# A half step of the frequency stage: all four products ahead of ScalarE's two copies

## The chip, the cores and the metric

One core of a Trainium2 chip runs the whole program in one launch. The metric is the device time of that launch in microseconds (us), the median of several runs. Engines are called by the names of the profile: PE is TensorE's matmuls (PEld its weight loads), DVE is VectorE, ACT is ScalarE, POOL is GpSimd, SP is SyncE, which issues most DMAs.

## The reference, cut to what matters

Two parts follow each other: a long convolution by Fourier transforms, and on its result a mixture of experts. The change lies in the first part:

```python
h_filt = h_mlp * window                       # S = 11456 positions, D = 128 channels
u = x * v                                     # B = 4 sequences
L = 2 * S
Uf = np.fft.rfft(u, n=L, axis=1)
Hf = np.fft.rfft(h_filt, n=L, axis=0)
y = np.fft.irfft(Uf * Hf[None, :, :], n=L, axis=1)[:, :S, :]
return (x * y).astype(np.float32)
```

Everything is float32. The second part (`_moe_ref`) picks rows of that result, sends each through one of 8 experts, and is not touched.

## The kernel before, in words

The transforms are matrix products. The sequence is cut into 3 blocks of 60 x 64 positions, and the 128 channels into 4 slices (`h`) of 32. A first stage (`first_phase`) transforms the filter and the data of slice 0 along 60 points and writes the results to DRAM (`x1f`, `x1d`). The frequency stage (`freq_phase`) reads them back. Its loop runs over 60 steps `n` (`ALL`), 15 for each slice, and every step treats four of the 60 frequencies, as two half steps `j` of two frequencies each.

One half step goes through four engines:

- `spread` (L385 to L399), called through `begin`: on PE, the products with the table `c2` take the data and the filter (`x1`, 480 columns) into frequency. There are four products of 64 output rows, two (`p` = 0, 1, which fill the lower and upper 64 partitions) for the real part (`c` = 0) and two for the imaginary part (`c` = 1). In the trace every one of them is two instructions of PE, so a group of two products is a row of "x4", two pairs that run side by side. Both groups write one PSUM tile `xp` of two banks, bank `c` for part `c`; there are two such tiles, `xp0` and `xp1`, one for each half step. ACT then copies each part to `xx` in SBUF (480 columns of the real, 384 of the imaginary part).
- `join` (L401): DVE adds the imaginary part in PSUM to the copied real part (L405), and forms the same sum of the filter (L407).
- `mult` (L410): DVE multiplies data with filter, three times (L414: `y`, `p1`, `p2`). It reads `xp` in PSUM, so the tile is free for the half step's next turn only behind the third.
- once per step, POOL adds `p1` and `p2` to `y` (L487, L488), and PE goes back from frequency (`back`, L429) one step later, in two parts (0 to 2, and 2 to 3, of the three blocks); ACT copies the result (L432), and SP stores it (`zd`, L441).

The data of the slices 1 to 3 goes through the first transform inside the frequency stage too, as pieces between the steps (`piece`, `others`): POOL multiplies x by v (L192), PE makes the products (L209), ACT copies them (L211) and issues the store to `x1d` (L197). The PSUM tiles `ps` of these pieces and of `back` come from one pool of four buffers (`qps`).

The order on each engine is the order in which the program is written (the schedule is manual); a layer that records tiles adds the waits on semaphores. On PE a step reads: `begin(n+1, 0)`, a piece, `back(0, 2)` of step n-1, `begin(n+1, 1)`, the other pieces that are due, `back(2, NB)`. The loads of `x1` (L381, L382) are issued by SP three steps ahead, into four buffers (`QX`). After the frequency stage the output stage (`out_phase`) makes the last transform, the routing and the experts.

Of the kernel before, what the change touches and what calls it, by code (L numbers as in the profile page):

```python
# [319 lines left out]
def freq_phase(tc, nc, i, fi, zd, c3, spare, loads):  # L320
# [9 lines left out]
    with (  # L330
# [9 lines left out]
        def c2(k, n=1):  # L340
            t, k = (spare, k) if k < HERE else (rest, k - HERE)
            return t[:, k * 128:(k + n) * 128]
# [42 lines left out]
        def spread(n, j):  # L385

            x1 = xs[n]
            xp = qpx.tile([128, 2, 512], F32, name=f"xp{j}")  # L390
            xx = qp.tile([128, NV, (NS + NB) * DH], F32, name=f"xx{j}", bufs=1)
            for c in range(2):
                for p in range(KH):
                    k = j * KH + p
                    nc.tensor.matmul(xp[p * 64:(p + 1) * 64, c, 0:(NS + NB) * DH],  # L395
                                     c2(n % PER * KS + k)[:, c * 64:(c + 1) * 64], x1[:, k], start=True, stop=True)
                w = (NS + NB * (1 - c)) * DH
                nc.scalar.copy(xx[:, 2 * c, 0:w], xp[:, c, 0:w])  # L398
            xps[n, j] = xp, xx  # L399
# [53 lines left out]
        def begin(n, j):  # L453
            if n < ALL:
                spread(n, j)
# [1014 lines left out]
```

## Time and profile before

| | us |
|---|---|
| median of 3 runs | 1673.21 |
| lowest and highest of them | 1672.59, 1675.7 |
| profiled execution, its own time | 1668.35 |
| its span, first to last instruction | 1666.6 |
| PE busy in that span | 1506.9 |
| DVE, POOL, ACT busy | 1059.1, 965.2, 805.6 |

The profile is one execution. The frequency stage stands from about 139 to 788 us in it. The queries used are the page itself, the waits of an engine (who stood still, and what ended it), the timeline (instructions in order of start), and windows (busy time of every engine in a stretch, with the clock granted to PE and the load of the DMA engines). In a timeline, the number in brackets is the idle time of the engine before the row and what ended it.

### The profile page before, as it was taken

How to read it: one execution, taken by the hardware profiler on the slowest of the kernel's cores; microseconds unless marked ns; L12 is line 12 of the kernel's file. 1: busy time of each engine (PE TensorE's matmuls, PEld its weight loads, DVE VectorE, ACT ScalarE, POOL GpSimd, SP SyncE). 2: the span in 40 equal slices, each digit the busy share in tenths (PEclk: the TensorE clock that was granted, in tenths of full speed). 3: DMA queues.
4: the chain of work that ended last, by engine and by line, in shares of the span. 5: the costliest groups of instructions: out<-in, count | busy, mean ns of one | idle time of the engine just before them, and what ended most of it. 6: DMA issues, size and time to landing. Idle time of an engine off the chain costs nothing. (4 is left out here: it accounts for less than half of the span.)

```text
span 1666.6 us, 27694 instructions
## 1 busy us (share of the span) xinstructions
PE 1506.9 (90%) x9149; PEld 891.9 (54%) x9149; DVE 1059.1 (64%) x2356; ACT 805.6 (48%) x1643; POOL 965.2 (58%) x808
## 2 busy tenths in 40 slices
PE   7994888888888888887789999999998999999997
PEld 3551333333333333233246776667676788888887
DVE  1324666666666667777386766667676877777773
ACT  4552554545545443333235455454544555555554
POOL 0103666666666655554036645953886788888755
PEclk9996999999999999999899999999999999999999
DMA  9999999999899988995797777877842111111100
GB/s 321 320 345 349 320 336 322 334 302 306 295 332 307 288 228 230 308 243 173 269 327 235 241 235 216 260 236 235 245 121 51 38 45 46 45 45 44 43 26 27
DMA packets 199255, 362.18 MB, mean 217 GB/s; under 512 B 64476, under 2 KB 138730, under 8 KB 199070
## 3 DMA queue, kind: packets, MB, share of 16 engines
q1 hardware_dynamic: 173430, 272.15, 50.5%
q10 hardware_dynamic: 10192, 52.51, 9.4%
q0 software_dynamic: 15488, 35.74, 7.6%
q8 instruction: 73, 1.20, 0.3%
q14 instruction: 72, 0.59, 0.1%
HBM read 216.89 MB, written 145.42 MB: 217 GB/s over the span
## 5 line engine op out<-in xcount | busy, mean ns | idle before, releaser
L740 POOL DMA_INDIRECT out<-o,ids x182 | 197.3, 1084 | 148.7 <-DVE o L747 112.2
L487 POOL TENSOR_TENSOR y<-y,p 128x1536 f32<-128x1536 f32 x59 | 203.3, 3445 | 117.4 <-DVE p L414 117.3
L429 PE MATMUL ps<-y,c 64*128 64x256 f32 (+1 forms) x1440 | 257.6, 488 | 0.4 <-POOL y L490 0.3
L669 POOL DMA_INDIRECT xt<-out,ids x182 | 192.2, 1056 | 48.4 <-issue 24.3
L398 ACT COPY xx<-xp 128x480 f32<-128x480 f32 x240 | 124.8, 520 | 176.7 <-PE xp L395 169.2
L405 DVE TENSOR_TENSOR xx<-xp,xx 128x384 f32<-128x384 f32 x120 | 66.9, 558 | 225.4 <-ACT xx L398 225.3
L882 DVE SCALAR_TENSOR_TENSOR hh<-hp,hh 128x1024 fp32r<-128x1024 f32 (+1 forms) x124 | 150.0, 1210 | 79.4 <-ACT hh L881 79.2
L429 PEld LDWEIGHTS ps<-y,c 64*128 64x128 f32 x1440 | 136.9, 186 | 114.2 <-issue 72.1
L395 PE MATMUL xp<-x,wf 128*64 128x480 f32 x512 | 135.3, 608 | 58.9 <-ACT xx L398 43.4
L432 ACT COPY z<-ps 128x512 f32<-128x512 f32 x240 | 103.6, 482 | 151.2 <-PE ps L429 151.2
L881 ACT ACTIVATE hh<-hp 128x1024 fp32r<-128x1024 f32 (+1 forms) x124 | 127.6, 1029 | 90.1 <-PE hp L736 87.1
L414 DVE TENSOR_TENSOR p<-xp,xx 128x768 f32<-128x768 f32 x240 | 169.3, 746 | 0.0
L192 POOL TENSOR_TENSOR wf<-wf 124x768 f32<-124x768 f32 x45 | 81.8, 1819 | 144.6 <-PE ps L209 109.6
L414 DVE TENSOR_TENSOR y<-xp,xx 128x1152 f32<-128x1152 f32 x120 | 162.8, 1357 | 4.1
L395 PE MATMUL xp<-x,c 128*64 128x480 f32 x448 | 114.9, 592 | 38.9 <-ACT xx L398 38.9
L211 ACT COPY wf<-ps 120x384 f32<-120x384 f32 x256 | 109.5, 486 | 47.2 <-PE ps L209 43.5
L1127 PE MATMUL y<-zt,c 128*64 128x512 f32 x384 | 110.6, 642 | 19.5 <-issue 11.0
L642 POOL MEMSET idle<- 128x512 f16 x226 | 122.5, 542 | 0.3
L209 PE MATMUL ps<-wf,c 60*120 60x384 f32 x512 | 118.5, 529 | 4.0 <-DVE wf L192 4.0
L824 PEld LDWEIGHTS bank<-wd,h 128*128 128x128 f32 x896 | 104.2, 191 | 32.8 <-issue 25.9
L620 POOL DMA_INDIRECT lists<-pl,lies x32 | 50.8, 1589 | 117.0 <-DVE step L1225 52.2
L824 PE MATMUL bank<-wd,h 128*128 128x128 f32 x896 | 114.5, 281 | 1.3 <-DVE o L747 1.3
(180 smaller groups left out, 2882.3 us busy)
## 6 DMA issues: line engine op xcount, KB each, us to landing
wf<-xv SPq DMA_DIRECT2D x64, 768.0 KB
x1d<-wf ACTq DMA_DIRECT2D x64, 720.0 KB
x<-x1d SPq DMA_DIRECT2D x60, 768.0 KB
zt<-zd SPq DMA_DIRECT2D x60, 768.0 KB
zd<-z SPq DMA_DIRECT2D x108, 384.0 KB
out<-xm SPq DMA_DIRECT2D x96, 258.0 KB
ox<-xo SPq DMA_DIRECT2D x96, 256.0 KB
x1f<-fx POOLq DMA_DIRECT2D x16, 720.0 KB
```

Of the source, the lines that this page charges most:

```text
L209: nc.tensor.matmul(ps[p], self.c1[rows], u[rows, q * RUN:(q + 1) * RUN], start=True, stop=True)
L395: nc.tensor.matmul(xp[p * 64:(p + 1) * 64, c, 0:(NS + NB) * DH], c2(n % PER * KS + k)[:, c * 64:(c + 1) * 64], x1[:, k], start=True, stop= ...
L398: nc.scalar.copy(xx[:, 2 * c, 0:w], xp[:, c, 0:w])
L414: nc.vector.tensor_tensor(o[:, :, j].rearrange("p v m b d -> p v (m b) d"), v[:, :, None, s * DH:(s + 1) * DH].broadcast_to([128, NV, m, DH]),
L429: nc.tensor.matmul(zps[p], c3[r, v], yv[r, v, :, lo:hi], start=(v == 0), stop=(v == NV - 1))
L487: nc.gpsimd.tensor_tensor(y[:, :, :, 1:], y[:, :, :, 1:], p1, ALU.add)
L642: self.nc.gpsimd.memset(self.idle, 0.0)
L669: ins = nc.gpsimd.indirect_dma_start(out=xt[:, j], out_offset=None, in_=self.rows[0:have], in_offset=bass.IndirectOffsetOnAxis(ap=ids[:, j ...
L740: ins = nc.gpsimd.indirect_dma_start(out=self.rows, out_offset=bass.IndirectOffsetOnAxis(ap=ids[:, j:j + 1], axis=0), in_=o, in_offset=Non ...
L824: nc.tensor.matmul(bank[:, j * D:(j + 1) * D], h[f // nf][:, k:k + 128], wd[u][:, f * D:(f + 1) * D], start=(f == 0), stop=(f == F // 128 ...
L881: nc.scalar.activation(v[:, 0], hp, AF.Relu)
L882: nc.vector.scalar_tensor_tensor(v[:, 1], hp, 0.0, v[:, 0].bitcast(F32), ALU.max, ALU.subtract)
```

## The change

The loop over the two parts is cut in two: `spread` issues the products of both parts, and only then the two copies. Nothing else is changed; every line below 396 moves down by one, so that L398 of before is L399 of after, L405 is L406, L414 is L415, L429 is L430.

```diff
             for c in range(2):
                 for p in range(KH):
                     k = j * KH + p
                     nc.tensor.matmul(xp[p * 64:(p + 1) * 64, c, 0:(NS + NB) * DH],
                                      c2(n % PER * KS + k)[:, c * 64:(c + 1) * 64], x1[:, k], start=True, stop=True)
+            for c in range(2):
                 w = (NS + NB * (1 - c)) * DH
                 nc.scalar.copy(xx[:, 2 * c, 0:w], xp[:, c, 0:w])
```

The sequence of instructions on each engine stays what it was. What the recording layer makes of it is another set of waits. On PE, at the second half step of a step of slice 0 (`xp_1883` is `xp1`, then the rows up to the next step's `xp_1922`), before:

```order
L395 MATMUL xp_1883<-x_1679,c_882 64x480 [waits DVE_49,PE_49]
L395 MATMUL xp_1883<-x_1679,c_882 64x480
L395 MATMUL xp_1883<-x_1679,c_882 64x480 [waits Activation_49]
L395 MATMUL xp_1883<-x_1679,c_882 64x480
L209 MATMUL ps<-wf,c_59 120x384 x2
L429 MATMUL ps<-y,c_61 128x2x128 [waits Pool_49]
L429 MATMUL ps<-y,c_61 128x2x128 x5
```

and after:

```order
L395 MATMUL xp_1883<-x_1679,c_882 64x480 [waits DVE_49,PE_49]
L395 MATMUL xp_1883<-x_1679,c_882 64x480 x3
L209 MATMUL ps<-wf,c_59 120x384 [waits Activation_49] x2
L430 MATMUL ps<-y,c_61 128x2x128 [waits Activation_49,Pool_49]
L430 MATMUL ps<-y,c_61 128x2x128 [waits Activation_49]
L430 MATMUL ps<-y,c_61 128x2x128 x4
```

The third product no longer waits for ACT; the products behind it (L209, L430) now name ACT themselves, for the copy that frees their PSUM buffer. On ACT and behind it on DVE, at the same half step, before (the rows of ACT first):

```order
L398 COPY xx_1884<-xp_1883 128x480 [waits DVE_49,PE_49]
L398 COPY xx_1884<-xp_1883 128x384 [waits PE_49]
L211 COPY wf<-ps 120x384 [waits PE_49] x2
L197 DMA x1d<-wf 120x1536 [waits DMAHW1_49,Activation_49]
L432 COPY z<-ps 128x2x128 [waits PE_49] x2
```

and after, ACT's two copies, and the first of DVE's five operations of the half step:

```order
L399 COPY xx_1884<-xp_1883 128x480 [waits DVE_49,PE_49]
L399 COPY xx_1884<-xp_1883 128x384
L211 COPY wf<-ps 120x384 [waits PE_49] x2
L197 DMA x1d<-wf 120x1536 [waits DMAHW1_49,Activation_49]
L433 COPY z<-ps 128x2x128 [waits PE_49] x2
...
L406 TENSOR_TENSOR xx_1884<-xp_1883,xx_1884 128x384 [waits PE_49,Activation_49]
```

The second copy has no wait of its own any more: the first one waits for all four products. DVE's sum (L405 before, with one wait on `Activation_49`) stands at the same place and waits for the second copy as before.

## Rows read from the trace of the kernel before

**Rows 1.** The page's busy times and two lines of its 40 slices: granted TensorE clock in tenths of full speed, and busy share of the DMA engines.
```profile
PE 1506.9 (90%) x9149; PEld 891.9 (54%) x9149; DVE 1059.1 (64%) x2356; ACT 805.6 (48%) x1643; POOL 965.2 (58%) x808
...
PEclk9996999999999999999899999999999999999999
DMA  9999999999899988995797777877842111111100
```

**Rows 2.** Waits of TensorE over the whole run: who waited for what, us in total, times, longest.
```profile
PE xp L395 <- ACT xx L398: 82.3, 120, 1.0
PE xp L395 <- DMA x<-x1d: 15.5, 1, 15.5
```

**Rows 3.** Timeline of TensorE in a step of the first stretch of the frequency stage, from one real group to that of the next step: start us, us, line, tiles, idle time before. A row of L395 is one group of two pairs.
```profile
404.47 1.03 PE L395 MATMUL xp<-x,c 128*64 128x480 f32 x4
406.15 1.03 PE L395 MATMUL xp<-x,c 128*64 128x480 f32 x4 [0.66 <-ACT xx L398]
407.11 0.91 PE L209 MATMUL ps<-wf,c 60*120 60x384 f32 x4
407.85 2.74 PE L429 MATMUL ps<-y,c 64*128 64x512 f32 x12
410.52 1.03 PE L395 MATMUL xp<-x,c 128*64 128x480 f32 x4
...
415.30 1.03 PE L395 MATMUL xp<-x,c 128*64 128x480 f32 x4
```

**Rows 4.** The same of a step of the second stretch, in which no data pieces are left.
```profile
671.96 1.03 PE L395 MATMUL xp<-x,wf 128*64 128x480 f32 x4
673.68 1.03 PE L395 MATMUL xp<-x,wf 128*64 128x480 f32 x4 [0.70 <-ACT xx L398]
674.64 2.85 PE L429 MATMUL ps<-y,c 64*128 64x512 f32 x12
677.42 1.03 PE L395 MATMUL xp<-x,wf 128*64 128x480 f32 x4
...
680.10 1.57 PE L429 MATMUL ps<-y,c 64*128 64x256 f32 x12
681.60 1.03 PE L395 MATMUL xp<-x,wf 128*64 128x480 f32 x4
```

**Rows 5.** Windows of line 395 alone: stretch, its us, PE busy (instructions), PEld busy (instructions), granted clock, DMA share, GB/s.
```profile
139.00:172.00 33.00, 16.39 (x50) 3.23 (x52) 0.76 1.02 356
172.00:602.00 430.00, 159.92 (x624) 30.70 (x622) 1.00 0.94 311
602.00:779.00 177.00, 73.87 (x288) 14.22 (x288) 1.00 0.80 229
```

**Rows 6.** Timeline of the same step as rows 4, ScalarE (ACT), VectorE (DVE) and GpSimd (POOL).
```profile
671.09 0.56 DVE L405 TENSOR_TENSOR xx<-xp,xx 128x384 f32<-128x384 f32 x1 [1.88 <-ACT xx L398]
...
673.07 0.56 ACT L398 COPY xx<-xp 128x480 f32<-128x480 f32 x1 [0.37 <-ACT z L432]
673.26 1.41 DVE L414 TENSOR_TENSOR p<-xp,xx 128x768 f32<-128x768 f32 x2
...
674.35 3.45 POOL L487 TENSOR_TENSOR y<-y,p 128x1536 f32<-128x1536 f32 x1 [4.30 <-DVE p L414]
...
674.76 0.48 ACT L398 COPY xx<-xp 128x384 f32<-128x384 f32 x1 [1.12 <-PE xp L395]
...
675.27 0.56 DVE L405 TENSOR_TENSOR xx<-xp,xx 128x384 f32<-128x384 f32 x1 [0.60 <-ACT xx L398]
...
677.87 1.81 POOL L488 TENSOR_TENSOR y<-y,p 128x768 f32<-128x768 f32 x1
```

**Rows 7.** Windows of eight whole steps of the first and of the second stretch: us, busy time of PE, PEld, DVE, ACT, POOL (instructions), granted clock, DMA share, GB/s.
```profile
339.40:426.10 86.70, 76.13 (x386) 29.43 (x384) 56.16 (x81) 43.38 (x96) 56.67 (x25) 1.00 0.94 305
...
662.30:739.70 77.40, 65.87 (x322) 23.53 (x320) 56.15 (x81) 29.99 (x64) 42.09 (x16) 1.00 0.95 284
```

**Rows 8.** Windows of the same form, just behind two short pauses of the DMA queue.
```profile
287.00:297.00 10.00, 9.34 (x48) 3.62 (x48) 6.18 (x10) 4.86 (x11) 7.03 (x3) 1.00 1.03 389
297.00:307.00 10.00, 8.68 (x48) 3.55 (x48) 6.18 (x10) 4.78 (x10) 6.44 (x3) 1.00 0.96 342
...
453.00:463.00 10.00, 8.68 (x48) 3.60 (x48) 6.78 (x10) 5.42 (x12) 6.24 (x4) 1.00 1.06 393
```

**Rows 9.** The line of the data products, L209: what ended the idle time of its engine before it (us, times), one row.
```profile
  ACT wf L211: 7.1, 7
```

**Rows 10.** Windows of the form of rows 7: the start of the frequency stage, the hand-over to the output stage, and a stretch of the output stage.
```profile
144.00:152.00 8.00, 6.50 (x16) 1.38 (x16) 2.80 (x4) 1.60 (x3) 0.00 (x0) 0.50 1.03 358
...
790.00:807.00 17.00, 7.75 (x16) 1.88 (x16) 1.55 (x3) 0.59 (x1) 0.00 (x0) 0.51 0.56 196
...
900.00:1220.00 320.00, 317.42 (x2688) 221.46 (x2685) 211.74 (x794) 160.07 (x415) 208.25 (x247) 1.00 0.77 238
```

**Rows 11.** Timeline of TensorE at the hand-over: the last products of the frequency stage and the first of the output stage.
```profile
785.70 1.89 PE L429 MATMUL ps<-y,c 64*128 64x512 f32 x14
798.41 3.33 PE L1127 MATMUL y<-zt,c 128*64 128x512 f32 x4 [10.82 <-issue]
```

**Rows 12.** Waits of SyncE's queue over the whole run, one row.
```profile
SPq L381 <- DMA x1d<-wf: 35.7, 6, 14.3
```

## The prediction

> **What bounds the kernel now.** I read the page first: PE is busy in 90% of the span, at a full granted clock nearly everywhere [rows 1]. So the next view is what PE waits for. One wait stands far ahead of all others: 82.3 us in 120 waits, always the products of L395 for ACT's copy L398; the wait for the loads of `x1` came once [rows 2]. There are 120 half steps, so every one of them pays it. The timeline shows where: between the real and the imaginary group PE stands still for 0.66 us [rows 3], or 0.70 us where no data pieces are left [rows 4], and nowhere else in the step: the real group, the pieces and `back` follow each other without a gap. PE's queue is thus the bound of the whole frequency stage, step by step: 415.30 - 404.47 = 10.83 us in the first stretch [rows 3], 681.60 - 671.96 = 9.64 us in the second [rows 4]. The pause has no purpose that the data asks for: the imaginary products write another bank of `xp` than the one being copied.
>
> **What the change removes.** The wait in the middle of a half step. I count from start to start, since the ends of matmuls are modelled. Now `spread` takes 407.11 - 404.47 = 2.64 us of PE [rows 3], and 674.64 - 671.96 = 2.68 us in the second stretch [rows 4]. Afterwards it is four pairs without a break, a form that the trace of before doesn't hold, so I bound it. From below: `back` does six pairs of 512 columns in 410.52 - 407.85 = 2.67 us [rows 3], 0.445 us each; for 480 columns that is 0.417 us, and four are 1.67 us. From above: the imaginary group takes 407.11 - 406.15 = 0.96 us for its two pairs, the passage to the next line included [rows 3]; twice that is 1.92 us. Only one of the two passages is left, so I take 1.78 us, between the two. A half step saves 2.64 - 1.78 = 0.86 us (0.72 to 0.97), in the second stretch 0.90 us (0.76 to 1.01). The least that could come is the visible idle time alone, 0.66 and 0.70 us.
>
> Eight instructions of L395 make a half step: 624 / 8 = 78 of them lie between 172 and 602 us and 288 / 8 = 36 behind; the first six run at a granted clock of 0.76 and beside the first loads [rows 5], and I give them 2 us in all. The sum is 78 x 0.86 + 36 x 0.90 + 2 = 67.1 + 32.4 + 2 = 101.5 us.
>
> **What it adds.** ACT's first copy now waits for four products instead of two, and its second copy follows at once. In the queue of ACT behind it stand the copies of the data piece and of `back` (L211, L432), which need products that PE makes later still, so they are not held up. DVE, which waits for the second copy, comes no later: now it starts 675.27 - 671.96 = 3.31 us after the first product [rows 4, 6]; then 1.78 us of products, a tail of about 0.1 us, and copies of 0.56 and 0.48 us [rows 6] make about 2.95 us.
>
> The products behind `spread` (L209, L429) get a wait of their own for the copy that frees their PSUM buffer. Four buffers serve two groups of two, so the copy asked for is two groups old and done, except where several data pieces follow each other; there PE already waited 7.1 us in 7 waits for L211 [rows 9]. Behind such a run PE now arrives earlier and waits longer. From 0 to another 7.1 us; I take 2 us.
>
> **What is late next.** Each engine has to fit into the shorter step. In the second stretch it becomes 9.64 - 1.80 = 7.84 us. DVE has 56.15 / 8 = 7.02 us of work in it [rows 7], a half step of DVE lasts 673.26 + 1.41 - 671.09 = 3.58 us [rows 6], two of them 7.16 us: it fits, with little to spare. POOL has 42.09 / 8 = 5.26 us there, and 56.67 / 8 = 7.08 us of 10.83 - 1.72 = 9.11 us in the first stretch [rows 7]. The turn of one `xp` tile (products 1.9, copies 1.04, DVE 3.58, some 0.1 for the signals) is 6.6 us, under both. POOL's sum for a step ends at 677.87 + 1.81 = 679.68 [rows 6], and the `back` that reads it starts behind the next step's first `spread`, at 681.60 + 2.68 = 684.28 us [rows 4]: 4.6 us early, of which three to four savings of 0.90 take 2.7 to 3.6. So no chain of the engines takes PE's place.
>
> The DMA engines are the open question. Their share is 0.94 in the first stretch, at 305 GB/s [rows 7]: 305 x 86.70 / 8 = 3.31 MB a step, or 3.31 MB / 9.11 us = 363 GB/s after the change. A share near 1 looks like a full queue, but behind two short pauses the same engines moved 389 and 393 GB/s over 10 us, at a share of 1.03 and 1.06 [rows 8]; and the loads are issued three steps ahead, which takes up short delays. I take the 363 GB/s as possible and give 1.5 us to places where loads come late: at the start of a slice SP waits for the last store to `x1d` (35.7 us in 6 waits, [rows 12]), and at the hand-over PE already idles 10.82 us [rows 11]. The Trainium skill speaks against this. Its page "DMA: Bandwidth & Descriptors" (section Specifications) gives about 358 GB/s as one core's share of HBM; by it, as an estimate, the 3.31 MB would take 9.24 us, 0.13 us a step more, some 5 us in all. The trace does not agree with it as a limit: 389 and 393 GB/s [rows 8].
>
> **The output stage** takes the gain over whole: PE is busy in 317.42 of its 320 us between 900 and 1220 us, at full clock [rows 10], and it begins when the frequency stage's last products are stored.
>
> So 101.5 - 2 - 1.5 = 98 us. The profiled execution took 1668.35 us, which makes 1570.4 us; the median of the three runs lies 4.9 us above it, and so does my forecast: 1673.2 - 98 = 1575 us.
>
> **The rivals.**
> - The DMA engines become the bound. For it: the share of 0.94 and 0.95 [rows 7]. If a share of 1.0 were the end and packets kept their times, a step of the first stretch could shrink only to 0.94 x 10.84 = 10.19 us and eight steps of the second to 0.95 x 9.68 = 9.19 us: 39 x 0.65 + 8 x 0.48 + 10 x 1.8 + 2 = 49 us, 1624 us. If instead 342 GB/s, the rate after the burst [rows 8], were the end, a step would be 9.67 us, 39 x 1.17 + 18 x 1.8 + 2 = 80 us, 1593 us. Against it: rows 8, and that PE never waits for a load in steady state [rows 2].
> - Only the visible idle time goes, because four pairs in a row need 1.92 us or more: 78 x 0.66 + 36 x 0.70 = 77 us less 3.5, 1600 us. Against it: `back` runs six pairs at 0.445 us [rows 3].
> - The wait moves instead of going: PE saves it in the middle and pays it at the next line, for ACT or DVE. Then the time stays at 1673 us. Against it: the new waits name copies two groups old, and DVE starts earlier.
> - Slower: loads that come late stop PE in every step, and the granted clock falls with it. The trace has this: after the 15.5 us wait for a load [rows 2] the clock was 0.50 [rows 10], after the 10.82 us at the hand-over 0.51 [rows 10, 11], the lower of the two levels (1.2 GHz). A step at half clock costs 9.1 us more; from 11 such steps on the gain of 98 us is gone, and with 20 of the 60 it is 182 - 98 = 84 us slower, 1757 us. It needs DMA engines far slower than the 305 GB/s they move now.
>
> **How the numbers follow.** Forecast (PE stays the bound) 0.70; only the idle time 0.10; DMA at 342 GB/s 0.08; DMA at its share 0.07; no change 0.03; slower 0.02. The range starts where the upper savings hold: 78 x 0.97 + 36 x 1.01 + 2 = 114 us, 1559 us, say 1560. It reaches up to 1603 us, past the cases of 1593 and 1600 us, and leaves out those of 1624 us and more with 0.12. About 0.2% (3.3 us) is what a measurement of this kernel can tell from no change. Faster takes all but the last two cases, 0.95; same 0.03; slower 0.02.
>
> **What would show it.** In the profile after: no wait of L395 for the copy (82.3 us before); the start of `spread` to the next line at 1.67 to 1.92 us; steps of about 9.1 and 7.8 us; DVE with idle times under 1 us in the second stretch; 360 GB/s in the first. I am wrong if PE's rows show waits for `x1` loads in each step (DMA), for DVE at the first product of a half step (then DVE is next), or for ACT at L209 and L430 (then the wait has moved).

## The result and the profile after

The changed kernel takes 1580.78 us (median of 4 runs, 1575.11 to 1583.72); the kernel before took 1673.62 us beside it (4 runs, 1672.59 to 1675.7). The ratio is 0.944, with an interval of [0.9411, 0.9468]. On another chip it was 0.9382 [0.9339, 0.9424], on a third 0.9364 [0.9324, 0.9404]. The profiled execution took 1575.11 us, 93.2 less than the one before; the forecast was 98 less.

The page: PE's share of the span went from 90% to 94%, with the same number of instructions [rows 1]. The third line is the rate of the DMA engines in the 40 slices, some 39 us each.

```profile
PE 1485.4 (94%) x9149; PEld 906.7 (58%) x9149; DVE 1057.4 (67%) x2356; ACT 790.3 (50%) x1643; POOL 963.8 (61%) x808
...
PEclk9996999999999999989899999999999999999999
DMA  8999999999999989969977687777521111111100
GB/s 319 316 335 339 364 390 371 377 360 363 359 390 361 301 230 359 316 218 344 314 237 227 218 240 243 246 233 234 152 57 39 36 46 45 46 45 44 41 28 24
```

PE's waits over the whole run. The row with 82.3 us [rows 2] is not there any more. The one wait for the loads of `x1` at the start is still there, and what is left for ACT in the steps is small:

```profile
PE xp L395 <- DMA x<-x1d: 15.9, 1, 15.9
...
PE ps L430 <- ACT wf L211: 2.6, 2, 2.1
```

The timeline of PE in a step of the first stretch answers to [rows 3]. A row of L395 is now all four pairs ("x8"), and no row has a bracket:

```profile
344.44 1.83 PE L395 MATMUL xp<-x,wf 128*64 128x480 f32 x8
346.20 0.91 PE L209 MATMUL ps<-wf,c 60*120 60x384 f32 x4
346.95 2.74 PE L430 MATMUL ps<-y,c 64*128 64x512 f32 x12
...
353.52 1.83 PE L395 MATMUL xp<-x,wf 128*64 128x480 f32 x8
```

From start to start `spread` takes 346.20 - 344.44 = 1.76 us where it took 2.64, and the step 353.52 - 344.44 = 9.08 us where it took 10.83. In the second stretch [rows 4] a step is now 599.16 - 591.36 = 7.80 us, 9.64 before:

```profile
591.36 1.83 PE L395 MATMUL xp<-x,wf 128*64 128x480 f32 x8
593.12 1.57 PE L430 MATMUL ps<-y,c 64*128 64x256 f32 x12
...
599.16 1.83 PE L395 MATMUL xp<-x,wf 128*64 128x480 f32 x8
```

Windows of eight steps of each stretch answer to [rows 7] (busy us of PE, PEld, DVE, ACT, POOL, then clock, DMA share, GB/s). PE is busy without a gap. The bytes of a step are the same, so the rate rose, from 305 to 352 and from 284 to 349 GB/s. (One of the eight steps in the first window is one of the four steps of the stage in which three data pieces follow each other. Such a step takes 11.62 us now and took 13.35; the window of before holds none. Over the five plain steps ahead of it, 344.40 to 389.80 us, the rate is 361 GB/s.)

```profile
344.40:419.60 75.20, 75.17 (x396) 32.11 (x394) 56.23 (x81) 42.82 (x100) 58.58 (x26) 1.00 0.99 352
591.40:653.70 62.30, 62.30 (x322) 24.93 (x320) 55.36 (x81) 28.83 (x64) 42.08 (x17) 1.00 1.04 349
```

Where the time came from is read from the first and the last start of a line. The products of `spread`, before:

```profile
L395 PE MATMUL xp<-x,wf x512: 566/617/1062, 144.2 to 708.5; 128*64 128x480 f32 x171
...
L395 PE MATMUL xp<-x,c x448: 566/592/617, 228.6 to 777.2; 128*64 128x480 f32 x150
```

and after:

```profile
L395 PE MATMUL xp<-x,wf x512: 566/566/1061, 145.5 to 623.8; 128*64 128x480 f32 x171
...
L395 PE MATMUL xp<-x,c x448: 566/566/823, 219.3 to 678.4; 128*64 128x480 f32 x150
```

The first products of the output stage, which began at 798.41 us before [rows 11]:

```profile
L1128 PE MATMUL y<-zt,c x384: 592/643/1116, 699.0 to 1128.0; 128*64 128x512 f32 x192
```

The frequency stage (first to last start of L395) went from 777.2 - 144.2 = 633.0 to 678.4 - 145.5 = 532.9 us, 100.1 less. The passage to the output stage went from 798.4 - 777.2 = 21.2 to 20.6 us. The first stage was 1.3 us longer. The output stage, to the end of the span, 1573.2 - 699.0 = 874.2 us where it had 1666.6 - 798.4 = 868.2, 6.0 us longer. Together: -100.1 - 0.6 + 1.3 + 6.0 = -93.4 us of span.

Step by step, from the first product of `spread` to that of the next step, 35 of the 39 steps of the first stretch save 1.74 to 1.76 us. The other four lie in slice 0 and save 5.2 us less than that together. The 39 steps give 63.5 us, the 18 of the second stretch 34.4 and the first three 2.3, which makes the 100.1 up to rounding.

### The profile page after: what moved, and what is told of

It is laid out like the page before. It is cut to its first block, busy times and chain, and to the rows that moved or that the text cites. A ratio compares the mean times of both kernels' runs of the same rounds, so it can differ in the third digit from the quotient of the medians.

```text
span 1573.2 us, 27965 instructions
## 1 busy us (share of the span) xinstructions
PE 1485.4 (94%) x9149; PEld 906.7 (58%) x9149; DVE 1057.4 (67%) x2356; ACT 790.3 (50%) x1643; POOL 963.8 (61%) x808
## 5 line engine op out<-in xcount | busy, mean ns | idle before, releaser
L430 PE MATMUL ps<-y,c 64*128 64x256 f32 (+1 forms) x1440 | 259.2, 490 | 4.1 <-ACT wf L211 2.6
L430 PEld LDWEIGHTS ps<-y,c 64*128 64x128 f32 x1440 | 138.9, 187 | 117.3 <-issue 83.0
L399 ACT COPY xx<-xp 128x480 f32<-128x480 f32 x240 | 112.9, 523 | 129.2 <-PE xp L395 97.5
L415 DVE TENSOR_TENSOR p<-xp,xx 128x768 f32<-128x768 f32 x240 | 169.3, 747 | 0.0
L415 DVE TENSOR_TENSOR y<-xp,xx 128x1152 f32<-128x1152 f32 x120 | 162.8, 1357 | 4.1
L406 DVE TENSOR_TENSOR xx<-xp,xx 128x384 f32<-128x384 f32 x120 | 66.7, 556 | 128.6 <-ACT xx L399 128.6
L395 PE MATMUL xp<-x,wf 128*64 128x480 f32 x512 | 120.9, 595 | 19.4 <-DMA x<-x1d 15.9
L1128 PE MATMUL y<-zt,c 128*64 128x512 f32 x384 | 109.2, 634 | 18.2 <-issue 10.5
L209 PE MATMUL ps<-wf,c 60*120 60x384 f32 x512 | 119.4, 530 | 3.2 <-DVE wf L192 2.7
L211 ACT COPY wf<-ps 120x384 f32<-120x384 f32 x256 | 111.2, 499 | 21.6 <-PE ps L209 12.6
L1129 DVE TENSOR_TENSOR xm<-y,ox 128x512 f32<-128x512 f32 x96 | 66.2, 689 | 69.1 <-PE y L1128 51.1
```

What stands on the lines that cost most here:

```text
L209: nc.tensor.matmul(ps[p], self.c1[rows], u[rows, q * RUN:(q + 1) * RUN], start=True, stop=True)
L415: nc.vector.tensor_tensor(o[:, :, j].rearrange("p v m b d -> p v (m b) d"), v[:, :, None, s * DH:(s + 1) * DH].broadcast_to([128, NV, m, DH]),
L430: nc.tensor.matmul(zps[p], c3[r, v], yv[r, v, :, lo:hi], start=(v == 0), stop=(v == NV - 1))
```

## The experiments

The theory is that of the prediction: PE's queue sets each half step, and the time gained is PE's pause between the two groups with one passage from row to row. The rivals ask whether ACT still matters, whether the copies have to be put together for it, whether it is the DMA engines that now set the step, and what caused the part that was lost. "Stage" below is the frequency stage in the profile, measured as above. All diffs are against the new kernel.

**The new kernel again.**

> The changed kernel once more, with more rounds. Theory (PE is the bound of the frequency stage, and the rest of the time follows it): the median stays at 1575 to 1584 us, about 0.944 of before, and the frequency stage in the new profile is as long as in the first one (about 533 us from the first product of L395 to its last) while the few us by which runs differ lie in the output stage. Rival (the runs differ because loads come late in the frequency stage): then that stage differs by several us between the two profiles, and PE shows waits for x1 loads in it.

1584.03 us, ratio 0.9382 [0.9339, 0.9424]. Stage 529.8 us (141.8 to 671.6), 3.1 less than in the first profile, while the output stage is 16.3 longer (below): most of the difference lies there, as the theory has it, and no step shows a wait for `x1`.

> The new kernel as it is, on the chip of the two runs with more loads: frequency stage 530 to 534 us as before, ratio 0.935 to 0.947.

1563.68 us, ratio 0.9364 [0.9324, 0.9404]. Stage 529.1 us (148.5 to 677.6). Thus three profiles of the new kernel give 529.1 to 532.9 us. The output stage is less steady: 1582.7 - 692.2 = 890.5 us in the run before and 1563.6 - 698.3 = 865.3 us in this one.

**The kernel before again.**

> The kernel before once more, for its profile. Theory (the few us by which runs of one kernel differ belong to the output stage, with or without the change): the frequency stage is 633 to 635 us long as in the first profile, whatever the run's time, and the output stage differs from the 861 us of the first profile by as much as the run differs. Rival (the change made the output stage longer): the output stage is at 859 to 864 us here too, whatever the chip.

1678.91 us, a single run. Stage 634.9 us (148.0 to 782.9), and an output stage of 1677.1 - 802.8 = 874.3 us. (By this measure the first profile has 868.2, not the 861 on record.) The rival is refuted: the kernel without the change has the longer output stage too. The theory holds in part only: of the 10.5 us by which the two spans differ, 6.1 are in the output stage, 3.8 ahead of the frequency stage and 1.9 in it, and the passage between them is 1.3 us shorter.

The other profiles tell what goes with that length. The output stage took 874.3 us on this chip, and there 872.5, 873.0 and 874.0 in the runs `piece_between`, `more_load` and `version` below, the last with the new order. On the chip of `after_same_chip` it took 865.3, 868.8 and 868.3 us in three runs, on that of `after_again` 880.7 to 898.2 in four. So it goes with the chip and not with the order of the copies. Why the chips differ stays open; the record doesn't name the chip of the first two profiles.

**The new order in one of the two half steps.** For `j` = 1 each copy is issued behind its own products again.

```diff
-            for c in range(2):
+                if j:
+                    w = (NS + NB * (1 - c)) * DH
+                    nc.scalar.copy(xx[:, 2 * c, 0:w], xp[:, c, 0:w])
+            for c in range(2 * (1 - j)):
                 w = (NS + NB * (1 - c)) * DH
                 nc.scalar.copy(xx[:, 2 * c, 0:w], xp[:, c, 0:w])
```

> Only the half step j = 0 gets the new order; j = 1 keeps a copy behind each group. Theory (PE is the bound, each half step gives its own wait back): half of the 93 us, 1627 us, 1619 to 1634; PE waits for the copy 60 times, 41 us. Rival (another engine takes over once one wait is gone): much less or nothing of the second half, so nearly all of the 93 us already here, 1580 to 1600 us. Rival (the other half step takes the wait over): 1665 us or more.

1636.38 us, ratio 0.9703 [0.9649, 0.9757]; stage 580.5 us (145.2 to 725.7), half the way. The time is 2.4 us above the expected range, which was reckoned from a chip on which the kernel before takes 1673 us; here it takes 1688.28, and half of the change gains 52 us of the 104 that the whole gains on this chip. PE's wait for the copy is back for 60 of the 120 half steps, with half of the 82.3 us:

```profile
PE xp L395 <- ACT xx L399: 41.4, 60, 1.0
```

Its timeline of PE holds both kinds side by side, 383.49 - 380.84 = 2.65 us in the old order, 387.39 - 385.62 = 1.77 in the new:

```profile
380.84 1.03 PE L395 MATMUL xp<-x,c 128*64 128x480 f32 x4
382.53 1.03 PE L395 MATMUL xp<-x,c 128*64 128x480 f32 x4 [0.66 <-ACT xx L399]
383.49 0.91 PE L209 MATMUL ps<-wf,c 60*120 60x384 f32 x4
...
385.62 1.83 PE L395 MATMUL xp<-x,c 128*64 128x480 f32 x8
387.39 0.91 PE L209 MATMUL ps<-wf,c 60*120 60x384 f32 x4
```

So the gain belongs to the single half step and adds up. No other engine ends it before PE does.

**More products.** The real part's two pairs run twice.

```diff
-            for c in range(2):
+            for c in (0, 0, 1):
                 for p in range(KH):
```

> The changed order with the real products made twice (the second time over the first, the same values): six pairs for a half step instead of four, nothing else. Theory (PE is the bound, a pair in an unbroken row costs 0.40 to 0.46 us): 120 x 0.80 to 0.92 = 96 to 110 us more than the changed kernel, 1677 to 1691 us, although no wait has come back. Rival (PE has room because DVE or the DMA engines are the bound now): less than 50 us more, under 1631 us.

1677.92 us, ratio 0.9933 [0.99, 0.9966]; stage 621.9 us (142.5 to 764.4), 92.1 more than the new kernel on the same chip. The time is as the theory has it, and two more pairs eat up nearly the whole gain. The timeline shows their price:

```profile
384.30 2.64 PE L395 MATMUL xp<-x,wf 128*64 128x480 f32 x12
386.86 0.91 PE L209 MATMUL ps<-wf,c 60*120 60x384 f32 x4
```

`spread` is 2.56 us here and 1.76 with four pairs: 0.40 us a pair, so 4 x 0.40 = 1.60 and 0.16 for the passage. The two old groups fit the same numbers: 2 x 0.40 + 0.16 = 0.96 us [rows 3]. The stage grew by less than the expected 96 us. The steps are 10.68 and 9.40 us, 1.61 longer, which is 96.6 us in 60; but the 3.3 us that the new kernel loses in slice 0 on this chip are not lost here, and the first three steps grew by 3.5 us instead of 4.8.

**More copies.** ACT makes the real copy twice.

```diff
-            for c in range(2):
+            for c in (0, 0, 1):
                 w = (NS + NB * (1 - c)) * DH
```

> The changed order with ACT's copy of the real part made twice: 0.5 us more of ACT in every half step, and DVE starts 0.5 us later. Theory (PE is the bound, the turn of an xp tile has over 1 us to spare): 0 to 8 us more, 1579 to 1589 us. Rival (the chain copy, DVE, next product is the bound now, or close to it): up to 120 x 0.5 = 60 us more; if only in the second stretch 36 x 0.5 = 18 us, 1599 us.

1589.35 us, ratio 0.9412 [0.9359, 0.9465], beside 0.9382 of the new kernel on that chip, the intervals overlap; stage 533.3 us (146.8 to 680.1), 3.5 more. ACT's three copies take 1.53 us in a row where the two took 0.94, so 120 x 0.59 = 71 us of ACT's time have been added, and they cost next to nothing: the steps are 9.07 and 7.79 us as in the new kernel, and 2.1 of the 3.5 us lie in the first three. ACT is off the path. Before the change ACT's copy was the path for 82.3 us.

**The old order of copies, with other work in the pause.** Each copy follows its own products, but a data piece or `back` stands between the real and the imaginary group.

```diff
-            begin(n + 1, 0)
+            begin(n + 1, 0, (0,))
             piece()
+            begin(n + 1, 0, (1,))
...
-            begin(n + 1, 1)
+            begin(n + 1, 1, (0,))
...
             piece(ALL)
+            begin(n + 1, 1, (1,))
```

(Cut: `spread` takes the parts as an argument, and has the copy behind each group as in the kernel before.)

> The old order of products and copies, each copy right behind its group, but the data piece stands between the real and the imaginary group (and behind it what follows), so that PE has other work while ACT copies. Theory (the wait costs what PE stands still; the distance between the two copies is of no account): in the first stretch, with pieces in nearly every half step, spread takes two groups of 0.96 us instead of 2.64, 78 x 0.6 to 0.72 = 47 to 56 us less in the frequency stage, 577 to 587 us instead of 633.6; nothing in the second stretch. Rival (the gain comes from copies back to back and an earlier start of DVE): no gain here, or a loss, since DVE starts 0.7 us later than before; 633 us or more.

1628.61 us, ratio 0.9721 [0.9677, 0.9765]; stage 587.7 us (145.9 to 733.6), 47.2 less than the kernel before on the same chip (634.9), at the rim of what was expected. PE still waits in the 38 half steps that have no piece to put there, 0.73 us each, and not in the others:

```profile
PE xp L398 <- ACT xx L401: 27.8, 38, 1.0
```

```profile
406.40 1.03 PE L398 MATMUL xp<-x,c 128*64 128x480 f32 x4
407.36 2.75 PE L209 MATMUL ps<-wf,c 60*120 60x384 f32 x12
410.05 1.03 PE L398 MATMUL xp<-x,c 128*64 128x480 f32 x4
411.00 1.57 PE L431 MATMUL ps<-y,c 64*128 64x256 f32 x12
```

Work in the pause takes the wait away. The copies need not follow each other for that, so the rival is refuted. But the second passage stays: 0.96 + 0.95 us for the four pairs where the new order needs 1.76, and the rows of the piece and of `back` are about 0.1 us longer each from start to start (0.84 for 0.74, 2.77 for 2.67). A plain step is 9.77 us, 1.07 less than before, where the new order has 9.07. Putting the four products together is better on both counts.

**More bytes, first try.** The filter's part of `x1` is loaded a second time into the same place.

```diff
+            nc.sync.dma_start(x1[:, :, fi.RUN:], fi.x1f[ks, :, :, h * w:(h + 1) * w].rearrange("k c n w -> (c n) k w"))
             return x1
```

> The changed order with the filter part of x1 loaded twice: 192 KB more for the DMA engines in each step, 0.20 MB on 3.31 MB, nothing for the other engines. Theory (the DMA engines are near their bound but not at it, and the loads lie three steps ahead): the frequency stage grows by 0 to 10 us from 530 to 533 us, and PE shows few waits for loads. Rival (the DMA engines are the bound beside PE): each step of the first stretch grows by 6%, 39 x 0.55 = 21 us, and in the second stretch some us more, with waits of L395 for x1.

1803.14 us, ratio 1.0762 [1.0706, 1.0818]; stage 757.9 us (147.1 to 905.0). This missed by far, and it says little about the bytes: the second load has to wait until the first has landed, in the queue of SP, and everything behind it stands.

```profile
SPq L383 <- DMA x<-x1f: 394.5, 60, 10.0
```

```profile
PE xp L396 <- DMA x<-x1f: 74.8, 27, 7.1
```

The transfers had room meanwhile: from 330 to 430 us their share was 0.79 at 249 GB/s, and the granted clock 0.91. This is much like the slower rival of the prediction, made by hand: loads that come late, PE that waits (22.70 of those 100 us it is idle), and a lower clock. The prediction held that this needs DMA engines far slower than before; loads that are issued late were enough.

**More bytes, free of that wait.** One more load of 192 KB, or of 768 KB, goes into a tile of its own that nothing reads. (The loads are issued once in a step, so there are 60 of them; the text on record says "half step" where it means the step of 9.07 us.)

```diff
+            extra = qx.tile([128, KS, NB * DH], F32, name="extra")
+            nc.sync.dma_start(extra, fi.x1f[ks, :, :, h * w:(h + 1) * w].rearrange("k c n w -> (c n) k w"))
```

For 768 KB the tile has three buffers and the load is that of `x1d[h][ks]`.

> The new kernel, and in each half step one more load of 192 KB of x1f into a tile of its own that nothing reads. Half steps of the first stretch last 9.07 us in the new kernel and slices of it show up to 390 GB/s. Theory (products set the half step, the loads still have room): frequency stage 0 to 10 us longer than in the new kernel (530 to 543 us), idle time of PE in it under 15 us. Rival (the loads already set the half step together with the products): each half step grows by the share that the load adds, some 6%, so 21 us or more in the stage, as waits of PE for x1d or x1f.

1600.37 us, ratio 0.9576 [0.9523, 0.9629]; stage 562.5 us (150.6 to 713.1), 33.4 more than the new kernel on the same chip. Neither text has it right: the size is the rival's, but the steps don't grow evenly, and PE hardly waits for loads. Windows of 40 us:

```profile
220.00:260.00 40.00, 34.22 (x162) 16.28 (x160) 21.97 (x33) 17.39 (x42) 24.83 (x11) 0.91 1.01 344
260.00:300.00 40.00, 33.39 (x160) 14.42 (x159) 22.62 (x32) 17.25 (x41) 24.41 (x11) 0.87 1.02 363
300.00:340.00 40.00, 40.00 (x218) 17.20 (x214) 30.13 (x45) 23.20 (x54) 31.50 (x15) 1.00 1.04 388
```

From 295 to 376 us every step keeps its 9.07 us with more bytes, so there the loads do not set it. But in slice 0, from 220 to 300 us, PE idles (40.00 - 34.22 and 40.00 - 33.39, 12.4 us) and works at 0.91 and 0.87 of the clock. Beside the new kernel on this chip 19.1 of the 33.4 us lie in eleven steps of slice 0, 6.8 in the last six steps, and the rest at the start and in the slices 1 and 2. PE's waits name ACT (L211 8.4 us, L435 8.2 us) and hardly the loads (3.1 us).

> The new kernel, and in each half step one more load of 768 KB of x1d into a tile of its own that nothing reads. Both theories expect the loads to be the bound here: some 4.1 MB per half step at 390 GB/s is 10.5 us where the products want 9.07, so the frequency stage grows by 55 to 110 us, and PE waits for x1d and x1f; the rate in its 40 slices then shows the most that the loads can move. If the stage grows by under 30 us, the transfers are further from a limit than either theory has it.

1656.89 us, ratio 0.9936 [0.9913, 0.996]; stage 621.2 us (143.1 to 764.3), 92.1 more, as both theories have it. From 495 to 588 us the transfers set the step:

```profile
500.00:540.00 40.00, 36.94 (x190) 17.79 (x187) 27.82 (x40) 19.03 (x47) 27.02 (x13) 1.00 1.04 393
540.00:580.00 40.00, 37.69 (x192) 18.66 (x192) 27.96 (x40) 19.51 (x46) 27.22 (x13) 1.00 1.04 392
```

```profile
491.32 1.83 PE L397 MATMUL xp<-x,wf 128*64 128x480 f32 x8
...
498.73 3.02 PE L432 MATMUL ps<-y,c 64*128 64x512 f32 x12 [0.84 <-ACT z L435]
501.68 1.83 PE L397 MATMUL xp<-x,wf 128*64 128x480 f32 x8
```

A step is 501.68 - 491.32 = 10.36 us at 392 GB/s, 4.06 MB, what 10.5 us at 390 GB/s had been put down for. Transfers that set the step thus move some 392 GB/s here, and the new kernel asks for 3.31 MB / 9.08 us = 365. The 392 are no hard end: from 420 to 460 us the new kernel itself shows 395 GB/s, and on the chip of this run

```profile
420.00:460.00 40.00, 40.00 (x212) 16.88 (x208) 31.42 (x46) 22.25 (x53) 31.10 (x13) 1.00 1.04 398
```

So the DMA engines don't bound the step, but they stand only some 7 to 9% behind PE. Again PE's waits name ACT's copies of `back` (36.1 us in 18 waits) more than the loads (12.7 us in 5, within the stage). In the step shown, the products that ACT has to copy end at 495.29 us, but ACT's queue stands at the store of a data piece (L197), which it issues at 497.85, and the copy comes at 498.21. So it is a store in ACT's queue that is late there, and the wait is shown at the copy behind it.

**What was lost in slice 0.** In the first profile of the new kernel four steps there are longer than others of their kind: 12.10 and 15.07 us where a step with three pieces in a row takes 11.62, 10.11 and 9.28 us where a plain one takes 9.07. This is PE at the end of the longest:

```profile
254.44 2.78 PE L209 MATMUL ps<-wf,c 60*120 60x384 f32 x12
259.35 3.30 PE L430 MATMUL ps<-y,c 64*128 64x256 f32 x12 [2.12 <-ACT wf L211]
262.58 2.03 PE L395 MATMUL xp<-x,c 128*64 128x480 f32 x8
```

and ACT, whose copies stand behind the issue of the store of a data piece (L197), which comes 258.39 - 255.39 - 0.88 = 2.1 us after the copies before it:

```profile
255.39 0.88 ACT L211 COPY wf<-ps 120x384 f32<-120x384 f32 x2
258.39 0.32 ACTq L197 DMA_DIRECT2D x1d<-wf  x1
258.81 1.63 ACT L211 COPY wf<-ps 120x384 f32<-120x384 f32 x4 [2.55 <-DMA zd<-z]
```

In slice 1 the same rows stand without a wait, from the three pieces at 396.75 us on:

```profile
399.55 1.94 PE L430 MATMUL ps<-y,c 64*128 64x256 f32 x12
401.43 1.83 PE L395 MATMUL xp<-x,c 128*64 128x480 f32 x8
```

From the pieces to the next `spread` it takes 262.58 - 254.44 = 8.14 us in the one and 401.43 - 396.75 = 4.68 in the other. Of the 3.46 us between them PE waits for 2.12. The rest is that the twelve products of L430 last 262.58 - 259.35 = 3.23 us for 401.43 - 399.55 = 1.88: behind the wait the granted clock is 0.55 from 259.30 to 262.60 us, nearly all of it the lower of the two levels (1.2 GHz). To see whether ACT's queue is the cause, SP issues these stores:

```diff
-            self.nc.scalar.dma_start(dst, xs)
+            self.nc.sync.dma_start(dst, xs)
```

> The new kernel with the stores of the data pieces (L197) issued by SyncE instead of ScalarE. In the profile of the new kernel ScalarE stands behind three such issues in slice 0, and PE loses 2.12 us and 0.59 us there with a drop of the clock, some 5 us in all. Theory (the loss comes from ScalarE's queue, which holds its copies until the store can be issued): PE's waits for L211 and L433 at L430 go, frequency stage 525 to 530 us. Rival (the loss comes from transfers that land late, whoever issues the store): SyncE's queue stands instead, and the loads behind it come later; frequency stage 530 to 545 us, with PE waiting for x1d, x1f or the sums of the data pieces.

1571.52 us, ratio 0.94 [0.9372, 0.9428]; stage 541.2 us (144.8 to 686.0), 8 to 12 longer. PE's waits for ACT are nearly gone (0.3 us). In their place SP stands, and what comes behind it in its queue is late:

```profile
SPq L197 <- ACT wf L211: 95.5, 35, 10.1
```

```profile
PE ps L209 <- POOL wf L192: 5.9, 3, 3.2
PE xp L395 <- DMA x<-x1f: 3.5, 5, 1.4
```

The waits and the length came as the rival has them, but its reason isn't shown. SP doesn't stand for late transfers here; it stands for ACT's copies, which make what is to be stored, and the loads behind come late by that. What is shown is that a queue that holds a store delays whatever stands behind it, on ACT as on SP. The whole time shows no difference that can be told from the new kernel's, which wasn't run on this chip.

**A version.** The data pieces spread more evenly over a step, and two more buffers for `z`:

```diff
-            z = qp.tile([128, KS, NS, DH], F32, name="z", bufs=4)
+            z = qp.tile([128, KS, NS, DH], F32, name="z", bufs=6)
...
-            piece()
+            piece(max(1, len(due) // 2))
```

> The changed order, with the pieces of a step dealt evenly over its two places (two and two where one and three stood), and six buffers instead of four for the result of back. Theory (what is left of PE's idle time in the frequency stage, some 5 us, comes from runs of three pieces and from copies that wait for stores to land): the frequency stage shrinks by 2 to 6 us, to 525 to 531 us. Rival (that idle time comes from late loads): it stays at 530 to 533 us. The median is about the changed kernel's less that, which the spread of the runs may hide.

1572.19 us, ratio 0.9374 [0.9338, 0.941]; stage 529.9 us (144.0 to 673.9), within the 529.1 to 532.9 us of the new kernel. No gain is shown, and the run doesn't tell theory from rival, whose ranges overlap there.

## Why the prediction was right

The forecast was 1575 us, from a saving of 98; the profiled execution shows 93.2 and the median 92.8. Nearly every term of the working can be put beside a row.

- **PE stays the bound: right.** The wait of 82.3 us is gone, and PE runs without a gap in eight steps of either stretch. The runs with one half step, with more products and with more copies show it from three sides: half the change gives half the gain, PE's work costs its price of 1.61 us in every step, and ACT's costs nearly nothing.
- **The price of four pairs, 1.78 us between 1.67 and 1.92: right, measured 1.76.** Its make-up was a little off. A pair takes 0.40 us, not the 0.417 scaled from `back`, and the passage 0.16. The upper bound, less one passage, would have been exact: 1.92 - 0.16 = 1.76. That the idle time alone would go is refuted: the half step saves 2.64 - 1.76 = 0.88 us, 0.66 of pause, 0.16 of passage and 0.06 more. Steps: 9.11 and 7.84 us forecast, 9.08 and 7.80 measured. The sum by the measured steps is 39 x 1.75 + 18 x 1.84 + 2 = 103.4 us, where 101.5 stood.
- **Losses of 2 us behind runs of pieces and 1.5 us by late loads: near in sum, and that in part by luck.** The stage gained 100.1 us, so 103.4 - 100.1 = 3.3 us are missing where 3.5 had been put down. But 5.2 us were lost in the four steps of slice 0. Some 2 us came back, 1.2 of them because four half steps late in the stage had waited 0.98 to 1.05 us before instead of 0.70, the rest by rounding and in the first three steps. The mechanism of the first term is there: behind a run of pieces PE waits for L211, 2.6 us in 2 waits. Its upper bound had no ground, though. The 7.1 us of [rows 9] are waits of the weight loads, 4.9 us of them ahead of the stage, and no row shows the matmuls of the kernel before waiting for L211 in the stage:

```profile
PEld ps L209 <- ACT wf L211: 7.1, 7, 3.6
```

What the lower clock adds (1.35 us in the longest step) was in neither term, and the late loads of the second term don't show: no step waits for `x1`. That the nearness of the transfers to their limit is behind the loss is supported from both sides. With 6% more bytes PE idled for 12.4 us in the same stretch and lost some of its clock. With the longer steps of the half change and of six pairs (9.96 and 10.68 us) no step of slice 0 with three pieces is longer than those of the later slices. Which transfer came late first was not told apart. The loss was 5.2, 3.3 and 2.0 us in three profiles of the new kernel.

- **The output stage takes the gain over whole: this term was off, by 6.0 us in the profiled execution.** It is the largest difference, and it makes the 98 into 93. The runs don't put it down to the change: on one and the same chip this stage takes 874.3 us with the old order and 874.0 with the new one (`version`), and from chip to chip it goes from 865 to 898 us. That the forecast of the time came within 6 us of the median thus rests in part on the chip.
- **What is late next: right.** DVE starts 602.05 - 599.16 = 2.89 us behind the first product in one half step, where 2.95 was forecast and 3.31 stood before. In the other, whose first product starts at 602.41, it comes straight from the half step before, 605.55 - 602.41 = 3.14 us behind. It still has some room: 55.36 of 62.30 us in eight steps, 6.92 us of 7.79 (forecast 7.02 of 7.84). This is its timeline in the second stretch, at the first operation of two half steps:

```profile
602.05 0.56 DVE L406 TENSOR_TENSOR xx<-xp,xx 128x384 f32<-128x384 f32 x1 [0.73 <-ACT xx L399]
...
605.55 0.55 DVE L406 TENSOR_TENSOR xx<-xp,xx 128x384 f32<-128x384 f32 x1
```

- **The DMA engines follow: right.** 349 to 352 GB/s over eight steps, 361 over five plain ones, and slices of 390. The rival by their share of 0.94 (1624 us) is refuted by the same windows: the share now reads 0.99 and 1.04, so a share near 1 said little about what was left. The rival of 342 GB/s (1593 us) is refuted too. The run with 768 KB more shows about what the prediction took from two windows of 389 and 393 GB/s [rows 8]: 392. The estimate by the Trainium skill ("DMA: Bandwidth & Descriptors", Specifications: about 358 GB/s for one core) of 0.13 us more in a step does not show; the trace does not agree with it as a limit of this core.

## What to carry to other kernels

A group of products that waits for a copy of another group's result, while it writes another bank of the same tile, is worth the pause and one passage on PE per turn; issue the groups together and copy behind them, and price it by start-to-start times of the timeline, not by the pause alone. Before it is counted, look at what each engine and the transfers have left in the shorter step: here DVE had 0.9 of 7.8 us and the transfers some 7 to 9%, so by these numbers a next saving on PE can't bring as much (no run tried one). And where transfers are near their limit, the wait can be shown on whatever queue is made to hold a store, and not on the load itself, as in the run with 768 KB.

## What was not expected of the hardware

- A second load into the same part of a tile, 192 KB, cost 394.5 us of SP's queue in 60 waits and made the kernel 7.6% slower than before the change, while the same bytes into a tile of their own cost 33.4 us of the stage.
- The transfers of this one core moved 388 to 398 GB/s for 40 us while PE was busy for all 40.00 of them, no less than the 392 to 393 where they set the step. The share of the DMA engines read 1.03 or 1.04 in all of these windows.
- ACT's copies of the two parts take 0.94 us together when they follow each other, where they started 1.69 us apart before [rows 6], and doubling the first one costs the stage 3.5 us.
